# Cached attention on one core: P times V in two 64-row tiles, V loaded with 2 KB rows, and banks shared with the query projection

## Chip, core and metric

The kernel runs on one core of a Trainium2 chip. The metric is the device time of one execution in microseconds. The engines are TensorE (PE, its weight loads listed apart as PEld), VectorE (DVE), ScalarE (ACT), GpSimd (POOL) and SyncE (SP), which issues the loads.

## What is computed

Two independent attention blocks A and B, with the same shapes, everything in bf16:

```python
B, Sq, D = 16, 64, 640
H, Sk, Dh = 32, 512, 128
...
q = (x @ wq).reshape(B, Sq, H, Dh).transpose(0, 2, 1, 3)
scores = jnp.einsum("bhqd,bhkd->bhqk", q, k_cache) * (Dh ** -0.5)
p = _softmax(scores, axis=-1)
o = jnp.einsum("bhqk,bhkd->bhqd", p, v_cache)
return o.transpose(0, 2, 1, 3).reshape(B, Sq, H * Dh) @ wo
```

The output is the two results side by side. Each K and each V cache holds 67 MB, so 268 MB of cache is read once.

## The kernel before

**Tiling.** A step is one head of two batches: 2 x 64 query rows fill the 128 partitions. Two steps (an even and an odd head of the same two batches) make a slot, with number m; there are 256. A group is 16 heads of two batches, 8 slots; a block's 32 heads are done in two passes, the second of which adds the sums of the first. Two slots share one chunk of K and one of V (4 heads), each loaded by two DMAs, one for each batch, into rings of five chunks.

**Stages of a slot**, by the names in the plan and the lines of the emitting code:

- KX (L433, PE): 8 transposes of K for each batch into the K bank; KE (L442, DVE) copies them to SBUF.
- QP2 (L451, PE): 10 matmuls, the query projection of both heads, into bank 6; QE2 (L459, ACT) copies it out, scaled.
- SM2 (L467, PE): 4 matmuls for the scores, each with a 64-column tile of the array, so that the two batches land on the two halves of the partitions. MX (L476, DVE) takes the maxima, EX (L482, ACT) the exponentials and their sums, RC2 (L488, DVE) the reciprocals.
- NM (L496, POOL): P times the reciprocal, one instruction for each head. TR2 (L505, PE): 8 transposes of P into bank 4; TE2 (L512, DVE) copies them out.
- PV2 (L524, PE): P times V, 16 matmuls with 128 keys each (2 heads x 2 batches x 4 key tiles) into bank 5; OE2 (L532, ACT) copies the result out.
- OP2 (L540, L545, PE): the output projection, which sums over a group's 16 heads in banks 0 and 1. At a group's end ACT copies the sum to SBUF (L555, first pass) or DVE adds it to the copy (L560, second pass), and ACT issues the store.
- XT (L604, PE) and XE (L612, ACT) transpose a group's x once, ten slots ahead, in bank 4.

**Order.** Nothing is scheduled at run time. Each engine runs a template once for each iteration k, and the number beside a stage says for which slot, k plus that number, it works:

```python
PE_T = (("TR2", 1), ("QP2", 4), ("KX", 4, 0), ("SM2", 3), ("PV2", 1), ("XT", 0), ("OP2", 0), ("KX", 4, 1))
ACT_T = (("QE2", 4), ("OE2", 1), ("XE", 0), ("EX", 3, 0), ("EX", 3, 1), ("OV", 0), ("ST", -1))
DVE_T = (("TE2", 1), ("RC2", 2), ("KE", 4, 0), ("MX", 3, 0), ("MX", 3, 1), ("KE", 4, 1), ("OVF", 0))
POOL_T = (("NM", 0, 0), ("NM", 0, 1))
```

So PE works on five slots at once. `make_op` lists for each stage the buffers and banks that it reads and writes; from these, in the order of the time stamps `ts`, the plan derives the dependencies, and `prune_waits` drops those that another wait implies. An instruction carries one wait itself; further ones stand as instructions of their own before it. The loads on SP are ordered once, by when their buffer comes free and by when they are due.

**Layout of keys.** K is loaded with 8 consecutive keys for each partition (2 KB in one piece), an even head on partitions 0 to 63 and the odd one on 64 to 127. V is loaded with 4 consecutive keys for each partition (1 KB), one head over all 128. So NM reorders the keys of P as it writes, with every second element, to fit V's order.

Of the kernel before, what the change touches and what calls it, by code (L numbers as in the profile page):

```python
# [14 lines left out]
class Cfg:  # L15
    G = 4
# [9 lines left out]
    NPN = 3  # L26
# [12 lines left out]
class Op:  # L39
# [3 lines left out]
    def __init__(self, eng, kind, idx, reads=(), writes=(), dur=0.0, ts=None, aux=None):  # L43
# [16 lines left out]
          "RC2", "NM0", "NM1", "TR2", "TE2", "XT", "XE", "PV2", "OE2", "OP2", "OV", "ST")  # L60
STAGE_IDX = {s: i for i, s in enumerate(STAGES)}
# [3 lines left out]
def build_plan(dims, cfg):  # L65
# [25 lines left out]
    def mk(eng, kind, idx, reads, writes, stage, m_ts, sub=0, aux=None, dur=0.0):  # L91
        return Op(eng, kind, idx, reads, writes, dur=dur, aux=aux, ts=(m_ts, STAGE_IDX[stage], sub))

# [4 lines left out]
    def make_op(kind, m, sub):  # L98
# [8 lines left out]
        if kind in ("MX", "EX", "NM"):  # L107
# [7 lines left out]
            return mk("pool", "NM", g, [("p", g % cfg.NP), ("recip", r)], [("pn", g % cfg.NPN)], "NM%d" % sub, m, sub)  # L115
        r0, r1 = g0 % cfg.NR, g1 % cfg.NR
        if kind in ("XT", "XE"):
# [4 lines left out]
            m_ts = mt - cfg.XLEAD + OFF["TR2"]  # L122
# [3 lines left out]
        if kind == "QP2":  # L126
            return mk("pe", "QP2", m, [("xT", grp % cfg.NX), ("wq", ps_ % 2, h0 // G)], [("QB",)], "QP2", m)
        if kind == "QE2":
            return mk("act", "QE2", m, [], [("QB",), ("qT", m % cfg.NQ)], "QE2", m)
# [5 lines left out]
        if kind == "TR2":  # L135
            return mk("pe", "TR2", m, [("pn", g0 % cfg.NPN), ("pn", g1 % cfg.NPN), ("ident",)], [("PTB",)], "TR2", m)
        if kind == "TE2":
            return mk("dve", "TE2", m, [], [("PTB",), ("pT", m % cfg.NT)], "TE2", m)
        if kind == "PV2":
            return mk("pe", "PV2", m, [("pT", m % cfg.NT), ("v", c % cfg.NVB, g0 % G), ("v", c % cfg.NVB, g1 % G)],  # L140
                      [("OB",)], "PV2", m)
        if kind == "OE2":
            return mk("act", "OE2", m, [], [("OB",), ("oT", m % cfg.NO)], "OE2", m)
        if kind == "OP2":
            return mk("pe", "OP2", m, [("oT", m % cfg.NO), ("wo", ps_ % 2, h0 // G)], [("OUTB",)], "OP2", m)
        if kind in ("OV", "OVF", "ST"):
# [3 lines left out]
            if kind == "OV":  # L150
                if NHALF == 1:
                    return mk("act", "OV", m, [], [("OUTB",), ("out_sb", grp % 2)], "OV", m, aux=grp)
# [3 lines left out]
            if kind == "OVF":  # L156
                if NHALF == 1 or not last_half:
                    return None
                return mk("dve", "OVF", m, [("outp", bp)], [("OUTB",), ("out_sb", grp % 2)], "OV", m, aux=grp)
            if NHALF == 1 or not last_half:  # L160
                return None
            return mk("act", "ST", m, [("out_sb", grp % 2)], [("out_dram", grp)], "ST", m, aux=grp)
# [3 lines left out]
    for eng, tmpl in templates.items():  # L166
        offs = [t[1] for t in tmpl] + [cfg.XLEAD]
        for k in range(-max(offs), NMAC - min(offs)):
            for t in tmpl:
# [8 lines left out]
                if 0 <= m < NMAC:  # L178
                    op = make_op(kind, m, sub)
                    if op is not None:  # L180
                        progs[eng].append(op)
                        if op.kind == "OV":
                            progs[eng].append(mk("act", "ST", m, [("out_sb", op.aux % 2)], [("out_dram", op.aux)],
# [7 lines left out]
    for ps_ in range(NPASS):  # L191
        first_m = ps_ * MPP
        buf = ps_ % 2
        for j in range(HG):
# [7 lines left out]
            loads.append((rq, m0 - OFF["QP2"], 0, mk("sp", "LDWQ", (ps_, j), [], [("wq", buf, j)], "LDW", m0,  # L202
# [3 lines left out]
    for grp in range(NGRP):  # L206
        m0 = MPG * grp
        op = mk("sp", "LDX", grp, [], [("xn", grp % cfg.NXN)], "LDX", m0 - cfg.XLEAD + OFF["TR2"], aux=grp,
# [35 lines left out]
    def sem_key(op):  # L244
# [6 lines left out]
        if op.kind == "ST":  # L251
            return ("d_out", op.aux % 2)
# [94 lines left out]
def mha_kernel(nc, blocks, out, cfg=None):  # L347
# [30 lines left out]
    with contextlib.ExitStack() as es:  # L378
# [11 lines left out]
        v_ring = sb("v_ring", [128, NVB, 2, G, 4, DH], BF16)  # L390
# [3 lines left out]
        pn_ring = sb("pn_ring", [128, NPN, SK], BF16)  # L394
        pT_ring = sb("pT_ring", [128, NT, 2, 4, 128], BF16)
        oT_ring = sb("oT_ring", [128, NO, 2, 128], BF16)
        out_sb = sb("out_sb", [128, 2, DN], BF16)
# [20 lines left out]
        pt_ps = pt_ps_flat.rearrange("p (s t q) -> p s t q", s=2, t=4)  # L418
        o_ps = ps[:, O_BANK, 0:256]
        q_ps = ps[:, Q_BANK, 0:256]  # L420
# [24 lines left out]
        def em_QP2(e, op):  # L445
            m = op.idx
            first = last = None
            for sub in range(2):
                blk, bp, grp, ps_, hh = step_info(2 * m + sub)
                for kt in range(KT):  # L450
                    ins = e.matmul(q_ps[:, sub * 128:(sub + 1) * 128], wq_sb[:, ps_ % 2, kt, hh * DH:(hh + 1) * DH],  # L451
# [5 lines left out]
        def em_QE2(e, op):  # L457
            m = op.idx
            ins = e.activation(qT_ring[:, m % NQ].rearrange("p s q -> p (s q)"), q_ps, ACTF.Copy, scale=scale)  # L459
# [31 lines left out]
        def em_NM(e, op):  # L491
            g = op.idx
            r = g % NR
            src = p_ring[:, g % NP, :].rearrange("q (th tl pp) -> q th tl pp", th=2, tl=4)
            dst = pn_ring[:, g % NPN, :].rearrange("q (tl pp th) -> q th tl pp", tl=4, th=2)
# [3 lines left out]
        def em_TR2(e, op):  # L499
            m = op.idx  # L500
            first = last = None
            for sub in range(2):
                g = 2 * m + sub
                for t in range(4):
                    ins = e.transpose(pt_ps[:, sub, t, :], pn_ring[:, g % NPN, t * 128:(t + 1) * 128], ident[:, :])  # L505
                    first = first or ins
                    last = ins
            return first, last

        def em_TE2(e, op):  # L510
            m = op.idx
            ins = e.tensor_copy(pT_ring[:, m % NT].rearrange("p s t q -> p (s t q)"), pt_ps_flat)  # L512
            return ins, ins

        def em_PV2(e, op):
            m = op.idx
            first = last = None
            for sub in range(2):
                g = 2 * m + sub
                c, gi = g // G, g % G  # L520
                for j in range(2):
                    for t in range(4):
                        col = sub * 128 + 64 * j
                        ins = e.matmul(o_ps[:, col:col + 64], v_ring[:, c % NVB, j, gi, t, :],  # L524
                                       pT_ring[:, m % NT, sub, t, 64 * j:64 * j + 64], start=(t == 0), stop=(t == 3))
# [4 lines left out]
        def em_OE2(e, op):  # L530
            m = op.idx
            ins = e.activation(oT_ring[:, m % NO].rearrange("p s q -> p (s q)"), o_ps, ACTF.Copy)  # L532
# [16 lines left out]
        def em_OV(e, op):  # L549
            ins = e.activation(out_sb[:, op.aux % 2, :], out_ps_all, ACTF.Copy)  # L550
# [7 lines left out]
        def em_OVF(e, op):  # L558
            blk, bp = grp_info(op.aux)
            ins = e.tensor_tensor(out_sb[:, op.aux % 2, :], out_ps_all, outp[:, bp, :], ALU.add)  # L560
            return ins, ins

        def em_ST(e, op):
            blk, bp = grp_info(op.aux)
            dst = out[2 * bp:2 * bp + 2, :, blk * DN:(blk + 1) * DN].rearrange("b q n -> (b q) n")
            ins = e.dma_start(dst, out_sb[:, op.aux % 2, :])
# [49 lines left out]
        def em_LDKV(e, op):  # L616
# [3 lines left out]
            if op.kind == "LDV":  # L620
# [99 lines left out]
```

## Time and profile before

| | |
|---|---|
| median of 2 runs | 959.13 us (958.80 to 959.47) |
| span of the profiled execution | 956.8 us |
| PE matmuls of KX, L433 | 4096, 220 ns each |
| of PV2, L524 | 4096 of 64 columns, 194 ns each |
| of SM2, L467 | 1024 of 512 columns, 392 ns each |
| ACT copies QE2 (L459) and OE2 (L532) | 256 each, 384 and 383 ns |
| POOL, L496 | 512, 843 ns each, 44% busy |
| DVE copies, L442 and L512 | 691 and 682 ns |
| moved by DMA | 299.51 MB, mean 313 GB/s |
| granted TensorE clock | 0.998 |

The mean duration of a matmul is not its cost: matmuls overlap in the array, and eight of 220 ns that start 56 ns apart are done after 0.61 us. What counts is the distance from start to start. Five slots are under way at once, so a wait names the instruction that came last, and a stage that ends well ahead of its reader costs nothing. The lines of the order of time give the start in us, the time from the first start to the last end, the engine, the line, what is written and read, and how many instructions were merged.

### The profile page before, as it was taken

What the parts mean: (1) busy time and instruction counts of PE and PEld (TensorE: products, weight loads), DVE (VectorE), ACT (ScalarE), POOL (GpSimd) and SP (SyncE); (2) the same over time, 40 slices, a digit from 0 to 9 for tenths busy, and PEclk for the clock granted to TensorE, in tenths of its full rate; (3) what the DMA queues carried; (4) which work ended last, traced back from release to release, by engine and by line L of the source; (5) the groups of instructions that cost most, each with busy time, mean ns of one, the idle gap of its engine ahead of it and who ended that gap; (6) DMA issues with size and microseconds to landing.
All of it is one profiled execution on the core that took longest, in us unless ns stands there. A gap on an engine that the chain in (4) does not pass through costs nothing.

```text
span 956.8 us, 34351 instructions
## 1 busy us (share of the span) xinstructions
PE 919.4 (96%) x14755; PEld 733.5 (77%) x15008; DVE 841.9 (88%) x1552; ACT 567.1 (59%) x1585; POOL 416.9 (44%) x518
## 2 busy tenths in 40 slices
PE   4999999999999999999999999999999999999997
PEld 3877777778777777877777787777877778777775
DVE  2898899898899999899999899889899998999996
ACT  1666656666665565656566666666666656565654
POOL 0444444444444444444444444444444444444443
PEclk9999999999999999999999999999999999999999
DMA  9999999999999999888999999988888988899830
GB/s 315 364 365 364 351 365 367 365 368 351 338 337 337 343 330 315 299 292 305 322 332 352 326 353 327 306 294 296 302 305 288 308 301 297 295 297 314 295 124 15
DMA packets 230871, 299.51 MB, mean 313 GB/s; under 512 B 9536, under 2 KB 165184, under 8 KB 230720
## 3 DMA queue, kind: packets, MB, share of 16 engines
q1 hardware_dynamic: 228416, 294.69, 91.0%
q8 instruction: 118, 1.93, 0.8%
q10 hardware_dynamic: 2304, 2.62, 0.8%
q14 instruction: 33, 0.27, 0.1%
HBM read 294.65 MB, written 2.62 MB: 311 GB/s over the span
## 4 chain that ended last, share of the span: by engine, by line
PE 89%; DVE 4%; POOL 3%; issue 2%; SPq 1%; DMA 1%; POOLq 0%; DVEq 0%
PE ps L433 22%; PE ps L524 14%; PE ps L451 14%; PE ps L467 14%; PE ps L505 12%; PE ps L545 7%; PE ps L540 5%; POOL pn_ring L496 3%; DVE out_sb L560 1%; DVE ktp_ring L442 1%; DVE pT_ring L512 1%; PE ps L604 1%; DMA xn_ring<-in_A_x_dram 1%; SPq L626 1%; SPq L583 1%
## 5 line engine op out<-in xcount | busy, mean ns | idle before, releaser
L496 POOL TENSOR_SCALAR pn_ring<-p_ring,recip 128x512 bf16<-128x512 bf16 x512 | 416.3, 843 | 532.7 <-DVE recip L488 532.7
L442 DVE COPY ktp_ring<-ps 128x1024 bf16<-128x1024 bf16 x512 | 353.7, 691 | 105.3 <-PE ps L433 85.1
L482 ACT ACTIVATE p_ring<-ps,negmax 128x512 bf16<-128x512 f32 x512 | 345.6, 684 | 4.8 <-DVE negmax L476 4.8
L476 DVE TENSOR_REDUCE negmax<-ps 128x1 f32<-128x512 f32 x512 | 327.3, 681 | 0.4 <-PE ps L467 0.3
L433 PE MATMUL ps<-ident,kn_ring 128*128 128x128 bf16 x4096 | 314.6, 220 | 2.8 <-DMA kn_ring<-in_A_k_cache_dram 1.6
L532 ACT ACTIVATE oT_ring<-ps 128x256 bf16<-128x256 f32 x256 | 98.0, 383 | 306.0 <-PE ps L524 306.0
L433 PEld LDWEIGHTS ps<-ident,kn_ring 128*128 128x128 bf16 x4096 | 251.9, 98 | 34.2 <-DVE ktp_ring L442 2.6
L524 PEld LDWEIGHTS ps<-pT_ring,v_ring 128*128 128x128 bf16 x4096 | 133.5, 98 | 109.2 <-issue 100.0
L451 PE MATMUL ps<-xT_ring,wq_sb 128*128 128x128 bf16 x2560 | 186.4, 220 | 3.2 <-DMA wq_sb<-in_A_wq_dram 3.2
L512 DVE COPY pT_ring<-ps 128x1024 bf16<-128x1024 bf16 x256 | 174.5, 682 | 4.6 <-PE ps L505 3.8
L524 PE MATMUL ps<-pT_ring,v_ring 128*128 128x64 bf16 x4096 | 163.8, 194 | 3.3 <-issue 1.7
L467 PE MATMUL ps<-ktp_ring,qT_ring 128*64 128x512 bf16 x1024 | 159.8, 392 | 0.4 <-ACT p_ring L482 0.4
L505 PE MATMUL ps<-ident,pn_ring 128*128 128x128 bf16 x2048 | 156.7, 219 | 3.5 <-POOL pn_ring L496 3.5
L451 PEld LDWEIGHTS ps<-xT_ring,wq_sb 128*128 128x128 bf16 x2560 | 155.2, 98 | 3.5 <-DMA wq_sb<-in_A_wq_dram 3.5
L459 ACT ACTIVATE qT_ring<-ps 128x256 bf16<-128x256 f32 x256 | 98.4, 384 | 66.8 <-PE ps L451 66.8
L505 PEld LDWEIGHTS ps<-ident,pn_ring 128*128 128x128 bf16 x2048 | 124.1, 98 | 7.0 <-POOL pn_ring L496 6.7
L545 PE MATMUL ps<-wo_sb,oT_ring 128*128 128x128 bf16 x512 | 112.1, 219 | 13.4
L482 ACT ACTIVATION_READ_ACCUMULATOR p_ring<-ps,negmax 128x1 f32 x512 | 105.0, 205 | 0.0
L540 PE MATMUL ps<-wo_sb,oT_ring 128*128 128x512 bf16 x259 | 97.8, 379 | 0.0
L540 PEld LDWEIGHTS ps<-wo_sb,oT_ring 128*128 128x128 bf16 x512 | 50.1, 98 | 30.6 <-ACT oT_ring L532 0.3
L467 PEld LDWEIGHTS ps<-ktp_ring,qT_ring 128*64 128x64 bf16 x1024 | 36.1, 108 | 27.1 <-ACT p_ring L482 0.6
L545 PEld LDWEIGHTS ps<-wo_sb,oT_ring 128*128 128x128 bf16 x512 | 50.1, 98 | 0.0
(13 smaller groups left out, 112.7 us busy)
## 6 DMA issues: line engine op xcount, KB each, us to landing
kn_ring<-in_A_k_cache_dram SPq DMA_DIRECT2D x128, 512.0 KB, 7.0
v_ring<-in_A_v_cache_dram SPq DMA_DIRECT2D x128, 512.0 KB, 7.2
kn_ring<-in_B_k_cache_dram SPq DMA_DIRECT2D x126, 512.0 KB, 4.8
v_ring<-in_B_v_cache_dram SPq DMA_DIRECT2D x126, 512.0 KB, 5.7
wq_sb<-in_A_wq_dram SPq DMA_DIRECT2D x8, 640.0 KB, 10.4
wo_sb<-in_A_wo_dram SPq DMA_DIRECT2D x8, 640.0 KB, 10.2
wq_sb<-in_B_wq_dram SPq DMA_DIRECT2D x8, 640.0 KB, 8.4
wo_sb<-in_B_wo_dram SPq DMA_DIRECT2D x8, 640.0 KB, 7.5
```

Source lines behind the costliest of these rows:

```text
L433: ins = e.transpose(kt_ps[:, t8, :], kn_ring[:, c % NKB, j, hp, t8, :], ident[:, :])
L442: ins = e.tensor_copy(dst, src)
L451: ins = e.matmul(q_ps[:, sub * 128:(sub + 1) * 128], wq_sb[:, ps_ % 2, kt, hh * DH:(hh + 1) * DH], xT_ring[:, grp % NX, kt, :], start=(kt ...
L467: ins = e.matmul(s_bank(sub)[64 * j:64 * j + 64, :], qT_ring[:, m % NQ, sub, 64 * j:64 * j + 64], ktp_ring[:, m % NKT, sub, j, :], start=T ...
L476: ins = e.reduce_max(negmax[:, r:r + 1], s_bank(g % 2), axis=AX.X, negate=True)
L482: ins = e.activation(p_ring[:, g % NP, :], s_bank(g % 2), ACTF.Exp, bias=negmax[:, r:r + 1], scale=1.0, accum_out=rowsum[:, r:r + 1])
L496: ins = e.tensor_scalar(dst, src, recip[:, r:r + 1], 1.0, ALU.mult, ALU.mult)
L505: ins = e.transpose(pt_ps[:, sub, t, :], pn_ring[:, g % NPN, t * 128:(t + 1) * 128], ident[:, :])
L512: ins = e.tensor_copy(pT_ring[:, m % NT].rearrange("p s t q -> p (s t q)"), pt_ps_flat)
L524: ins = e.matmul(o_ps[:, col:col + 64], v_ring[:, c % NVB, j, gi, t, :], pT_ring[:, m % NT, sub, t, 64 * j:64 * j + 64], start=(t == 0), s ...
L540: ins = e.matmul(out_ps0, oT_ring[:, m % NO, sub, :], wo_sb[:, ps_ % 2, hh, 0:N0], start=(hh == 0), stop=(hh == SPB - 1))
L545: last = e.matmul(out_ps1, oT_ring[:, m % NO, sub, :], wo_sb[:, ps_ % 2, hh, N0:DN], start=(hh == 0), stop=(hh == SPB - 1))
```

## The change

V is laid out as K is: 8 consecutive keys for each partition, an even head on partitions 0 to 63 and the odd head on 64 to 127. P is normalised into a tile that holds both heads, for each of 8 key tiles 64 keys of the one beside 64 of the other, so that one transpose serves both heads. P times V then runs with 64 keys for each matmul: 32 matmuls instead of 16, alternating between the upper half (even head) and the lower half (odd head) of the array, each named by `tile_position`. The two halves write different banks, 5 and 6; for that the query projection and P times V share both banks, one head in each, and each of the two stages now waits until the other's result was copied out. The output buffer shrinks from two to one, pn becomes two buffers of two heads, and the time stamps count from the reference stage of each part of the pipeline.

```diff
-    NPN = 3
+    NPN = 2
...
+TSREF = dict(KX0="QP2", KE0="QP2", KX1="QP2", KE1="QP2", QP2="QP2", QE2="QP2", LDK="QP2", SM2="SM2", MX0="SM2",
+             MX1="SM2", EX0="SM2", EX1="SM2", RC2="SM2", NM0="SM2", NM1="SM2", TR2="TR2", TE2="TR2", PV2="PV2",
+             OE2="PV2", LDV="PV2", OP2="OP2", OV="OP2", ST="OP2")
...
     def mk(eng, kind, idx, reads, writes, stage, m_ts, sub=0, aux=None, dur=0.0):
+        if stage not in ("LDX", "XT", "XE"):
+            m_ts = m_ts - OFF.get(TSREF.get(stage), 0) + (stage in ("RC2", "NM0", "NM1"))
...
-            return mk("pe", "QP2", m, [("xT", grp % cfg.NX), ("wq", ps_ % 2, h0 // G)], [("QB",)], "QP2", m)
+            return mk("pe", "QP2", m, [("xT", grp % cfg.NX), ("wq", ps_ % 2, h0 // G)], [("QOB",)], "QP2", m)
...
-            return mk("act", "QE2", m, [], [("QB",), ("qT", m % cfg.NQ)], "QE2", m)
+            return mk("act", "QE2", m, [], [("QOB",), ("qT", m % cfg.NQ)], "QE2", m)
...
-                      [("OB",)], "PV2", m)
+                      [("QOB",)], "PV2", m)
...
-            return mk("act", "OE2", m, [], [("OB",), ("oT", m % cfg.NO)], "OE2", m)
+            return mk("act", "OE2", m, [], [("QOB",), ("oT", m % cfg.NO)], "OE2", m)
...
-        v_ring = sb("v_ring", [128, NVB, 2, G, 4, DH], BF16)
+        v_ring = sb("v_ring", [128, NVB, 2, G // 2, 8, DH], BF16)
...
-        pn_ring = sb("pn_ring", [128, NPN, SK], BF16)
-        pT_ring = sb("pT_ring", [128, NT, 2, 4, 128], BF16)
+        pn_ring = sb("pn_ring", [128, NPN, 8, 2, 64], BF16)
+        pT_ring = sb("pT_ring", [128, NT, 8, 128], BF16)
...
-        out_sb = sb("out_sb", [128, 2, DN], BF16)
+        out_sb = sb("out_sb", [128, 1, DN], BF16)
...
-        o_ps = ps[:, O_BANK, 0:256]
-        q_ps = ps[:, Q_BANK, 0:256]
+        pt_ps = pt_ps_flat.rearrange("p (t q) -> p t q", t=8)
+        qo_ps = ps[:, O_BANK:Q_BANK + 1, 0:128]
...
-            src = p_ring[:, g % NP, :].rearrange("q (th tl pp) -> q th tl pp", th=2, tl=4)
-            dst = pn_ring[:, g % NPN, :].rearrange("q (tl pp th) -> q th tl pp", tl=4, th=2)
+            src = p_ring[:, g % NP, :].rearrange("q (t pp) -> q t pp", t=8)
+            dst = pn_ring[:, (g // 2) % NPN, :, g % 2, :]
             ins = e.tensor_scalar(dst, src, recip[:, r:r + 1], 1.0, ALU.mult, ALU.mult)
...
-            for sub in range(2):
-                g = 2 * m + sub
-                for t in range(4):
-                    ins = e.transpose(pt_ps[:, sub, t, :], pn_ring[:, g % NPN, t * 128:(t + 1) * 128], ident[:, :])
+            for t in range(8):
+                ins = e.transpose(pt_ps[:, t, :], pn_ring[:, m % NPN, t].rearrange("q h p -> q (h p)"), ident[:, :])
...
-            for sub in range(2):
-                g = 2 * m + sub
-                c, gi = g // G, g % G
-                for j in range(2):
-                    for t in range(4):
-                        col = sub * 128 + 64 * j
-                        ins = e.matmul(o_ps[:, col:col + 64], v_ring[:, c % NVB, j, gi, t, :],
-                                       pT_ring[:, m % NT, sub, t, 64 * j:64 * j + 64], start=(t == 0), stop=(t == 3))
+            c, hp = 2 * m // G, (2 * m % G) // 2
+            for j in range(2):
+                for t in range(8):
+                    for sub in range(2):
+                        r0 = 64 * sub
+                        ins = e.matmul(qo_ps[:, sub, 64 * j:64 * j + 64], v_ring[r0:r0 + 64, c % NVB, j, hp, t, :],
+                                       pT_ring[r0:r0 + 64, m % NT, t, 64 * j:64 * j + 64],
+                                       start=(t == 0), stop=(t == 7), tile_position=(r0, 0))
...
-            if op.kind == "LDV":
-                src = blocks[blk][2][2 * bp + j, h0 + hlo:h0 + hhi].rearrange("g (p t) d -> p g t d", p=128)
-                ins = e.dma_start(v_ring[:, c % NVB, j, hlo:hhi], src)
-            else:
...
+            cache, ring = (blocks[blk][2], v_ring) if op.kind == "LDV" else (blocks[blk][1], kn_ring)
+            src = cache[2 * bp + j, h0 + hlo:h0 + hhi].rearrange("(hp hs) (p t) d -> (hs p) hp t d", hs=2, t=8)
+            ins = e.dma_start(ring[:, c % NKB, j, hlo // 2:hhi // 2], src)
```

## The prediction

> **What bounds the kernel now.** I read the page first, in the order busy shares, chain, groups; then the waits; then the instructions in order of time between 400 and 412 us.
>
> ```profile
> PE 919.4 (96%) x14755; PEld 733.5 (77%) x15008; DVE 841.9 (88%) x1552; ACT 567.1 (59%) x1585; POOL 416.9 (44%) x518
> ...
> PE 89%; DVE 4%; POOL 3%; issue 2%; SPq 1%; DMA 1%; POOLq 0%; DVEq 0%
> ...
> L524 PEld LDWEIGHTS ps<-pT_ring,v_ring 128*128 128x128 bf16 x4096 | 133.5, 98 | 109.2 <-issue 100.0
> ...
> L467 PEld LDWEIGHTS ps<-ktp_ring,qT_ring 128*64 128x64 bf16 x1024 | 36.1, 108 | 27.1 <-ACT p_ring L482 0.6
> ...
> kn_ring<-in_A_k_cache_dram SPq DMA_DIRECT2D x128, 512.0 KB, 7.0
> v_ring<-in_A_v_cache_dram SPq DMA_DIRECT2D x128, 512.0 KB, 7.2
> ```
>
> PE is on 89% of the chain that ended last. A busy PE alone would not prove that the array is full, so the order of time decides:
>
> ```profile
> 400.26 0.64 PE L524 MATMUL ps<-pT_ring,v_ring 128*128 128x64 bf16 x16
> ...
> 400.74 0.44 PE L604 MATMUL ps<-ident,xn_ring 128*128 128x128 bf16 x5
> ...
> 403.01 0.61 PE L433 MATMUL ps<-ident,kn_ring 128*128 128x128 bf16 x8
> ...
> 403.21 0.38 ACT L459 ACTIVATE qT_ring<-ps 128x256 bf16<-128x256 f32 x1
> ...
> 403.55 0.62 PE L467 MATMUL ps<-ktp_ring,qT_ring 128*64 128x512 bf16 x4
> ...
> 404.10 0.52 PEld L524 LDWEIGHTS ps<-pT_ring,v_ring 128*128 128x128 bf16 x16 [0.41 <-issue]
> 404.11 0.64 PE L524 MATMUL ps<-pT_ring,v_ring 128*128 128x64 bf16 x16
> ...
> 404.79 0.38 ACT L532 ACTIVATE oT_ring<-ps 128x256 bf16<-128x256 f32 x1 [1.19 <-PE ps L524]
> ...
> 405.13 0.61 PE L433 MATMUL ps<-ident,kn_ring 128*128 128x128 bf16 x8
> 405.58 0.61 PE L505 MATMUL ps<-ident,pn_ring 128*128 128x128 bf16 x8
> ...
> 405.97 0.60 PEld L451 LDWEIGHTS ps<-xT_ring,wq_sb 128*128 128x128 bf16 x10
> ...
> 407.12 0.62 PE L467 MATMUL ps<-ktp_ring,qT_ring 128*64 128x512 bf16 x4
> ```
>
> From L467 to the next L467 is 407.12 - 403.55 = 3.57 us: one slot, two heads of two batches. L433 starts every (0.61 - 0.219)/7 = 0.056 us; eight make 0.45, and L505 follows exactly 405.58 - 405.13 = 0.45 later. So between full-array groups the array has no gap. L524 starts every (0.64 - 0.193)/15 = 0.029-0.030 us; sixteen make 0.47, and L604 follows 0.48 after it: no gap either. But L433 to L467 is 403.55 - 403.01 = 0.54, which is 0.45 plus a gap of 0.09. L467's second pair starts at 0.62 - 0.38 = 0.24, and its 512 columns take 0.22 (L540 to L545, 401.29 to 401.51), so the array is free at 404.01 and L524 starts at 404.11: a gap of 0.10. Nothing is late there: the weights' idle time is "issue". These two gaps are where 64-column tiles begin and end.
>
> Whole run: 3.57 x 256 = 914; 30 slots with L604 add 0.28 each, 8; 16 slots with the vector add L560 stretch their two periods to 404.11-407.86-411.75, that is 3.75 and 3.89, 0.5 more than twice 3.57, 8 in all. Head and tail make the rest of the 956.8 us span. The median of the runs is 959.1, 2.3 above the span; I carry that difference over. Each 0.01 us a slot is 2.5 us, counting 250 slots (the first are paced by loads, the last three by the softmax chain).
>
> **The change part by part.** *P-times-V matmuls.* 16 matmuls of 128 rows become 32 of 64 rows, in pairs on the upper and lower half of the array; each still streams 64 columns. If a pair runs side by side, 16 pairs keep the 0.029 pace and the block stays 0.47. L467 shows side-by-side tiles: within the first 0.41 us after 403.55 lie two of its 512-column matmuls, though one alone lasts 0.39. That is for column halves; row halves no row shows. Each pair also needs two weight loads of 128 columns. The trace's first two L524 loads end 0.11 apart from the first's start, so the second began 0.11 - 0.098 = 0.015 after the first; two, one after the other, are 0.03 a pair, just the pace of the matmuls. I add 0.013 for the block. Bounds: 0 if the loads hide; a gain is excluded, since a half-array tile streams as many columns; above, no overlap, 32 x 0.0292 = 0.93, +0.47.
>
> The Trainium skill, "TensorE: Matmul & The Clock Gate", Part 3, gives about 4 ns between starts of packed tiles; by it, as an estimate, a pair would cost 0.033 and the total would be some 13 us higher than mine. Its Weight-path section ties the fast weight load to 128 columns, not to rows, which no run here shows for a 64-row tile.
>
> *A third change of tile shape.* Before, PE goes full, columns, full: two gaps a slot, 0.09 and 0.10. After, it goes full, columns, rows, full: PV2 to OP2 (or XT) is new. The nearest rows are these two gaps, so I take 0.095, plus 0.010 because the first load can no longer run ahead (L524's first matmul lasts 203 ns instead of 193): 0.105 a slot. Lower bound 0, if only column tiles cost it; a gain is excluded, as PV2 to OP2 has no gap now. This is the largest term.
>
> "TensorEngine Tiling (Array Packing)", Key Properties, says that changing the tiling mode, not just the tile, drains the engine; it speaks against the change and gives no figure. By it the new gap must come, and with the measured size the sum is mine; without it the sum is the second case below.
>
> *Shared banks.* QP2 now waits for OE2, with KX0, SM2 and all behind it in PE's queue. OE2 ends 404.79 + 0.38 = 405.17, QP2 starts 405.97: 0.80 spare. PV2 waits for QE2, with OP2, KX1 and TR2 behind it: QE2 ends 403.21 + 0.38 = 403.59, PV2 starts 404.10: 0.51 spare. In slots where ACT copies partial sums at L555, QE2 ends at 59.56 and PV2 starts at 59.85: 0.29 spare. Cost 0; without the spare each 0.1 us late is 25 us. QE2 and OE2 now read two banks; same size, 0.38 each, ACT is 59% busy.
>
> *The normalising (NM).* Its writes become runs of 64 instead of every second element. POOL takes 2 x 0.81 a slot and is 44% busy; I take no change. A gain is worth at most the 8 us of the L560 slots, where PE waits for it; slower by over 0.24 us a slot (it ends 405.28, TR2's loads start 405.52) it would enter the loop. TR2 and TE2 keep 8 transposes and one copy.
>
> *V's transfers.* As many DMAs of the same 512 KB, 2 KB per row as K has now: median 7.0 us to landing against 7.2. PE waits for DMAs only at the start, some 12 us in all. Gain 0 to 1, I take 0; a V load slower than K's would have five chunks of cover.
>
> *One answer together:* the output buffer goes from two to one (a store lands in 5.6 us, the next group comes after eight slots, 28 us), two buffers of pn for pairs replace three singles, and the time stamps change only the order in which dependencies are found: 0. If the output buffer's cover were gone, 16 stores of 5.6 us bound it.
>
> *Given back.* In L560 slots DVE is the late one (0.81 more on 3.50 of work in 3.57). Slots longer by 0.118 give back 2 x 0.118 x 16 = 4 us.
>
> Sum: 0.105 + 0.013 = 0.118 x 250 = 29.5; minus 4; 956.8 + 25.5 + 2.3 = 985. With a pair at 0.030 to 0.040 instead, and the gap 0.09 to 0.105, the span of this case is 975 to 1028.
>
> **The rivals.** *The gap is the column tiles' own (not slower).* Both gaps now touch L467, and L467's 64-column load lasts 108 ns against 98 for 128 columns, so it is the odd one. If row tiles cost no gap, 0.013 x 250 = 3, minus up to 8 from L560 slots if NM gets quicker: 953 to 962. It decides once the new gap is under 0.06 (0.073 x 250 - 2 = 16). Against it: the second gap stands before full-array work, whose loads were free to run ahead.
>
> *The halves do not overlap, or loads go slowly.* Serial matmuls cost 0.93 a block. So do slow loads: L467's take about 0.03 for 64 columns (0.14 busy for four, less 0.108), hence 0.06 for 128, times 16 = 0.93. So does the queue, if it cannot pass PE's instructions faster than L524's 32 in 0.47, since there are now 64. All give (0.47 + 0.105) x 250 = 143, less the 8: 1094. For it: no row shows 64-row tiles. Against: L467's pairs overlap, and its four instructions start within 0.01.
>
> *QE2 ends last before PV2.* If ACT took 0.1 more than its spare, 1010. Against: 0.51 spare in nearly all slots.
>
> *PE gets shorter* would need fewer streamed columns; nothing removes any.
>
> **How the numbers follow.** Third gap with overlapping halves 0.58; no gap 0.20; no overlap 0.17; late QE2 0.03; faster for a reason not seen 0.02. About 2% (19 us, to 978) is what a measurement can tell. Slower by over 2%: 0.54 of the first (its low end falls inside), 0.17 and 0.03: 0.74. Within: 0.20 + 0.04 = 0.24. Faster: 0.02. The range takes the first two cases and the late QE2, 953 to 1028, some 0.80, and leaves out no overlap and faster. The likeliest case's own range is 975 to 1028.
>
> **What would show it.** A slot of 3.68 to 3.70 us; a gap of about 0.1 between the last PV2 matmul and L545's group; PV2's 32 matmuls within 0.65, starting in pairs; no wait of PE for ACT; periods at L560 slots only 0.3 above two slots. PV2 lasting 1.1 us would make the sum wrong by the third case; a slot of 3.57 to 3.60 by the second; PE waiting for oT_ring or qT_ring would show the shared banks.

## The result, and the profile after

| | before | after |
|---|---|---|
| median | 959.13 us | 989.55 us (986.73 to 992.36, 2 runs) |
| ratio | | 1.0315 [1.0284, 1.0346] |
| span of the profiled execution | 956.8 us | 985.0 us (device time 986.73) |
| distance from L467 (after: L472) to the next, normal slot | 3.57 us | 3.67 us |
| POOL, NM | 843 ns | 695 ns |
| share of the load queue q1 in the DMA engines' time | 91.0% | 85.3% |

Slower by 3%, and slower by the route that the forecast took. From the page of the kernel after: busy time by engine, the queues, the chain that ended last, three groups and two DMA issues.

```profile
PE 959.3 (97%) x19104; PEld 748.4 (76%) x19104; DVE 842.2 (86%) x1552; ACT 571.1 (58%) x1585; POOL 349.9 (36%) x518
...
q8 instruction: 151, 2.47, 1.0%
...
PE 93%; DVE 3%; SPq 1%; issue 1%; DMA 1%; POOL 0%; POOLq 0%; ACT 0%; DVEq 0%
...
L501 POOL TENSOR_SCALAR pn_ring<-p_ring,recip 128x512 bf16<-128x512 bf16 x512 | 349.3, 695 | 627.8 <-DVE recip L493 627.8
...
L526 PEld LDWEIGHTS ps<-pT_ring,v_ring 64*128 64x128 bf16 x8192 | 134.4, 95 | 111.6 <-issue 104.6
...
L472 PEld LDWEIGHTS ps<-ktp_ring,qT_ring 128*64 128x64 bf16 x1024 | 36.1, 108 | 27.2 <-ACT p_ring L487 0.6
...
kn_ring<-in_A_k_cache_dram SPq DMA_DIRECT2D x128, 512.0 KB, 5.5
v_ring<-in_A_v_cache_dram SPq DMA_DIRECT2D x128, 512.0 KB, 6.3
```

PE's share of the chain rose from 89 to 93%: no other engine became the bound. The loads got easier and land sooner, and nothing waits for that. PE's busy time rose by 40 us, which says little: it is the union of overlapping records, and the records before were a few per cent short (14755 of 15008 matmuls). One slot in order of time says more:

```profile
402.24 0.62 PE L472 MATMUL ps<-ktp_ring,qT_ring 128*64 128x512 bf16 x4
402.80 0.64 PE L526 MATMUL ps<-pT_ring,v_ring 64*128 64x64 bf16 x32
403.37 0.39 PE L543 MATMUL ps<-wo_sb,oT_ring 128*128 128x512 bf16 x1
403.60 0.22 PE L548 MATMUL ps<-wo_sb,oT_ring 128*128 128x128 bf16 x1
...
405.92 0.62 PE L472 MATMUL ps<-ktp_ring,qT_ring 128*64 128x512 bf16 x4
406.47 0.64 PE L526 MATMUL ps<-pT_ring,v_ring 64*128 64x64 bf16 x32
407.04 0.39 PE L543 MATMUL ps<-wo_sb,oT_ring 128*128 128x512 bf16 x1
```

The 32 matmuls of 64 rows (L526) take the 0.64 us that the 16 of 128 rows took. In the single records two start 3 ns apart and the next two 29 ns after these, 0.450 us from the first start to the last, against 0.447 before. But L543 starts 0.57 after the block's start. From L526's last start to L543's is 0.122; before, 0.029 was enough from L524 to L604 (in most other slots the record of the first L540 is missing). That is the third gap, 0.093 us. L543's first matmul lasts 390 ns instead of 379, 0.010 more. L545's records are all there, and they say the same of a slot without L604: before, its first matmul starts 0.69 after the block's start (404.11), after (L548) 0.80.

```profile
404.80 0.22 PE L545 MATMUL ps<-wo_sb,oT_ring 128*128 128x128 bf16 x1
```

The other two changes of shape are as they were: 149 ns from the last of K's transposes to the scores, 312 ns from the last score matmul to P-times-V. The normal slot grew by 0.107 us, 3.674 instead of 3.567.

This, 252 times, makes 27.0 of the 28.2 us that the span grew by. The rest has two parts, both in PE's row. The first is an idle PE that waits for no semaphore ("issue"), here after L548:

```profile
133.97 0.38 PE L543 MATMUL ps<-wo_sb,oT_ring 128*128 128x512 bf16 x1
134.19 0.22 PE L548 MATMUL ps<-wo_sb,oT_ring 128*128 128x128 bf16 x1
135.27 0.62 PE L438 MATMUL ps<-ident,kn_ring 128*128 128x128 bf16 x8 [0.86 <-issue]
```

From L548 to L438 is 0.056 elsewhere; here it is 1.08. There are 13 such stalls, 0.2 to 1.0 us each, 5.7 us together, and none before. The instruction at which PE goes on has the same number each time, counted from PE's first and modulo 256. A 16 KB packet of the instruction queue q8 started 2.2 to 2.7 us ahead of each. 256 instructions in 16 KB are 64 bytes for one, and the 151 packets of q8 (118 before) go with PE's 38208 matmuls and weight loads (2 x 15008 = 30016 before). So I read these stalls as PE at the end of a page of instructions whose successor isn't there yet; the median distance from one 16 KB packet to the next is 6.4 us instead of 7.8.

The second part goes the other way. Before, a slot with the vector add lost 0.18 at P-times-V (behind TE2) and 0.32 at TR2 (behind NM). After, it loses 0.27, all at P-times-V, and again behind TE2 (L515), which follows the vector add (L563) on DVE:

```profile
898.74 0.81 DVE L563 TENSOR_TENSOR out_sb<-ps,outp 128x640 bf16<-128x640 f32 x1
...
899.14 0.39 ACT L464 ACTIVATE qT_ring<-ps 128x256 bf16<-128x256 f32 x1 [0.37 <-PE ps L456]
899.48 0.68 DVE L515 COPY pT_ring<-ps 128x1024 bf16<-128x1024 bf16 x1
...
900.30 0.64 PE L526 MATMUL ps<-pT_ring,v_ring 64*128 64x64 bf16 x32 [0.20 <-DVE pT_ring L515]
```

TE2 ends at 900.16, just ahead of P-times-V; QE2 (L464) was done at 899.53. The view of the waits has two lines that look alike (us, times, longest):

```profile
PEld ps L526 <- ACT qT_ring L464: 6.6, 16, 0.4
...
PE ps L526 <- DVE pT_ring L515: 3.0, 15, 0.2
```

The first lies in 15 slots with ACT's copy of the first pass and one at the start. Its 0.41 is the idle time that any L526 load has, so QE2 costs nothing there. The second is the loss. Fifteen slots with 0.24 less give 3.6 us back (the sixteenth addition falls in the tail). Head, first three slots and tail are 1.0 shorter. Together 27.0 + 5.7 - 3.6 - 1.0 = 28.1 of 28.2.

### The profile page after: what moved, and what is told of

It reads as the page before. It is cut to its first block, busy times and chain, and to the rows that moved or that the text cites. A ratio compares the mean times of both kernels' runs of the same rounds, so it can differ in the third digit from the quotient of the medians.

```text
span 985.0 us, 42919 instructions
## 1 busy us (share of the span) xinstructions
PE 959.3 (97%) x19104; PEld 748.4 (76%) x19104; DVE 842.2 (86%) x1552; ACT 571.1 (58%) x1585; POOL 349.9 (36%) x518
## 3 DMA queue, kind: packets, MB, share of 16 engines
q1 hardware_dynamic: 162880, 294.69, 85.3%
## 4 chain that ended last, share of the span: by engine, by line
PE 93%; DVE 3%; SPq 1%; issue 1%; DMA 1%; POOL 0%; POOLq 0%; ACT 0%; DVEq 0%
PE ps L438 22%; PE ps L526 15%; PE ps L456 14%; PE ps L543 14%; PE ps L472 13%; PE ps L508 11%; PE ps L548 3%; PE ps L607 1%; DVE out_sb L563 1%; DVE ktp_ring L447 1%; DVE pT_ring L515 1%; DMA xn_ring<-in_A_x_dram 1%; SPq L625 1%; SPq L586 0%; POOL pn_ring L501 0%
## 5 line engine op out<-in xcount | busy, mean ns | idle before, releaser
L501 POOL TENSOR_SCALAR pn_ring<-p_ring,recip 128x512 bf16<-128x512 bf16 x512 | 349.3, 695 | 627.8 <-DVE recip L493 627.8
L438 PE MATMUL ps<-ident,kn_ring 128*128 128x128 bf16 x4096 | 314.7, 220 | 4.0 <-DMA kn_ring<-in_A_k_cache_dram 1.5
L438 PEld LDWEIGHTS ps<-ident,kn_ring 128*128 128x128 bf16 x4096 | 251.8, 98 | 36.0 <-DVE ktp_ring L447 2.6
L526 PEld LDWEIGHTS ps<-pT_ring,v_ring 64*128 64x128 bf16 x8192 | 134.4, 95 | 111.6 <-issue 104.6
L515 DVE COPY pT_ring<-ps 128x1024 bf16<-128x1024 bf16 x256 | 174.4, 681 | 4.3 <-PE ps L508 4.3
L526 PE MATMUL ps<-pT_ring,v_ring 64*128 64x64 bf16 x8192 | 164.7, 191 | 5.6 <-DVE pT_ring L515 3.0
L543 PE MATMUL ps<-wo_sb,oT_ring 128*128 128x512 bf16 x512 | 169.0, 384 | 0.0
L472 PE MATMUL ps<-ktp_ring,qT_ring 128*64 128x512 bf16 x1024 | 159.9, 392 | 0.4 <-DVE ktp_ring L447 0.4
L464 ACT ACTIVATE qT_ring<-ps 128x256 bf16<-128x256 f32 x256 | 98.7, 385 | 87.9 <-PE ps L456 87.9
L548 PE MATMUL ps<-wo_sb,oT_ring 128*128 128x128 bf16 x512 | 112.1, 219 | 0.5 <-issue 0.4
L543 PEld LDWEIGHTS ps<-wo_sb,oT_ring 128*128 128x128 bf16 x512 | 49.7, 97 | 41.8 <-ACT oT_ring L535 0.2
L472 PEld LDWEIGHTS ps<-ktp_ring,qT_ring 128*64 128x64 bf16 x1024 | 36.1, 108 | 27.2 <-ACT p_ring L487 0.6
L548 PEld LDWEIGHTS ps<-wo_sb,oT_ring 128*128 128x128 bf16 x512 | 50.3, 98 | 0.7 <-issue 0.7
## 6 DMA issues: line engine op xcount, KB each, us to landing
wo_sb<-in_A_wo_dram SPq DMA_DIRECT2D x8, 640.0 KB, 10.3
```

Of the source, the lines that this page charges most:

```text
L438: ins = e.transpose(kt_ps[:, t8, :], kn_ring[:, c % NKB, j, hp, t8, :], ident[:, :])
L472: ins = e.matmul(s_bank(sub)[64 * j:64 * j + 64, :], qT_ring[:, m % NQ, sub, 64 * j:64 * j + 64], ktp_ring[:, m % NKT, sub, j, :], start=T ...
L501: ins = e.tensor_scalar(dst, src, recip[:, r:r + 1], 1.0, ALU.mult, ALU.mult)
L515: ins = e.tensor_copy(pT_ring[:, m % NT].rearrange("p t q -> p (t q)"), pt_ps_flat)
L526: ins = e.matmul(qo_ps[:, sub, 64 * j:64 * j + 64], v_ring[r0:r0 + 64, c % NVB, j, hp, t, :], pT_ring[r0:r0 + 64, m % NT, t, 64 * j:64 * j ...
L543: ins = e.matmul(out_ps0, oT_ring[:, m % NO, sub, :], wo_sb[:, ps_ % 2, hh, 0:N0], start=(hh == 0), stop=(hh == SPB - 1))
```

## The experiments

**The theory.** Each change between full-array, column and row tiles costs PE about 0.09 us, and 64-row matmuls pair up without loss. Rivals: the gap is the column tiles' own, or belongs to the end of the P-times-V block; the shared banks or the loads cost part of it. Beside these: what the stalls are, and what the change holds that is worth keeping.

**The kernel after once more** (no edit), to see whether the stalls are fixed in place.

> The changed kernel once more, for its spread. Its profile shows twelve stalls of PE of 0.2 to 1.0 us in places without a wait, 5.7 us in all, and before shows none; its two runs lie 5.6 us apart, those of before 0.7. If the stalls are late instructions that depend on what the load traffic does in each run, the runs lie between 984 and 994 and differ by several us, and the stalls are in other places in this profile. If they belong to places in the program, the stalls come back in the same places and the runs lie within 1 us.

989.19 us (986.07 to 994.93, 4 runs), ratio 1.0318 [1.0282, 1.0355]. The profile had 15 stalls, 7.7 us, in a device time of 989.31; after's had 5.7 in 986.73. So 2.0 of the 2.6 us between the two executions are stalls. Nine of the 15 came at the same ends of pages as in the first profile, the others at other ends, and all at the same number modulo 256: the places where a stall can come are fixed, whether one comes is not. The runs of the kernel before lay within 1.8 us (7 runs), these within 9.

**One full-array matmul at the end of the block**, and **the same matmul between its two batches**. It streams 8 columns and writes columns that nothing reads.

```diff
+            last = e.matmul(ps[:, O_BANK, 256:264], ident[:, :], pT_ring[:, m % NT, 0, 0:8], start=True, stop=True)
```

```diff
+                if j == 0:
+                    e.matmul(ps[:, O_BANK, 256:264], ident[:, :], pT_ring[:, m % NT, 0, 0:8], start=True, stop=True)
```

> The changed kernel plus one matmul of 8 columns on the full array after the 32 tiled ones of P times V, with the same number of changes of tile shape a slot (three). All theories: the small matmul costs about 0.03 us a slot, 250 x 0.03 = 7 us, so 992 to 1000. It is the control of the next run; its result goes to an unused part of bank 5 and is not read.

> The same small matmul, but in the middle of the 32 tiled ones, between the two batches: the array goes rows, full, rows, two more changes of shape a slot. Each change costs 0.094 plus 0.010 for the load that cannot run ahead (my theory): 0.21 a slot more than the control, +52 us, about 1048. Rival one, the 0.094 belongs to the end of the P times V block, whatever its shape: the same time as the control within 5 us. Rival two, only column tiles cost a change: also the same as the control.

At the end: 997.50 us, ratio 1.0404 [1.0385, 1.0424]. In the middle: 1036.85 us, 1.0813 [1.0794, 1.0832]. One slot of each in order of time, first the matmul (L531) at the end:

```profile
404.00 0.64 PE L526 MATMUL ps<-pT_ring,v_ring 64*128 64x64 bf16 x32
404.57 0.18 PE L531 MATMUL ps<-pT_ring,ident 128*128 128x8 bf16 x1
404.61 0.38 PE L544 MATMUL ps<-wo_sb,oT_ring 128*128 128x512 bf16 x1
```

then the matmul (L532) in the middle:

```profile
400.24 0.41 PE L526 MATMUL ps<-pT_ring,v_ring 64*128 64x64 bf16 x16
400.58 0.18 PE L532 MATMUL ps<-pT_ring,ident 128*128 128x8 bf16 x1
400.69 0.41 PE L526 MATMUL ps<-pT_ring,v_ring 64*128 64x64 bf16 x16
401.03 0.39 PE L545 MATMUL ps<-wo_sb,oT_ring 128*128 128x512 bf16 x1
```

At the end the gap stands ahead of L531, 0.122 from the last L526, and next to none is left before L544 (0.039 instead of 0.029). In the middle the last L526 of a batch to L532 is 0.122, L532 to the next L526 is 0.112, and the end keeps its 0.122. The work is the same; two more changes of shape lengthen the slot from 3.70 to 3.89, 0.19 us (I had written 0.21). That is 0.095 for each change, in a place that has nothing to do with the column tiles or the end of the block: both of those rivals are out. Over 250 slots 0.191 makes 48; the profiled spans differ by 45.0, with 3.3 us less in stalls. The medians differ by 39.4: the profiled execution with the matmul at the end was the fastest of its four, the one with it in the middle the slowest.

"TensorEngine Tiling (Array Packing)" in the Trainium skill, Key Properties, says that changing the mode drains TensorE; these two runs agree, in that PE loses time at each change, and give it a price here, 0.083 to 0.095 us.

**The two row halves one after the other.** Eight key tiles of the upper half, then eight of the lower.

```diff
-                for t in range(8):
-                    for sub in range(2):
+                for sub in range(2):
+                    for t in range(8):
```

> The changed kernel with the 32 tiled matmuls in another order: for each batch all eight of the upper half, then all eight of the lower half, so that neighbours share a half. If two matmuls run side by side only when neighbours use different halves, the block grows from 0.47 to 0.92 or 0.93 us, +0.45 x 250 = +113, about 1102. If the two halves run side by side in any order, 985 to 994. If the alternation had not bought anything, also no change.

1024.53 us, ratio 1.068 [1.0659, 1.0701]: slower, but far less than the 1102 that I wrote down. The block in order of time:

```profile
401.78 0.81 PE L526 MATMUL ps<-pT_ring,v_ring 64*128 64x64 bf16 x32
402.52 0.39 PE L543 MATMUL ps<-wo_sb,oT_ring 128*128 128x512 bf16 x1
```

From the first to the last start it takes 0.617 us, not the 0.905 of 32 in single file, nor the 0.450 of pairs. The single starts are 0, 39, 69, 98, 127, **135**, 156, **174**, 185, **203**, 214 ns and on: two strands with 29 ns steps, of which the second begins while the first is still in its eight. The records don't name the half. But steps under 29 ns are seen in no other P-times-V block than those that alternate halves, so the second strand must be the lower half's: its first matmul starts before three of the upper half's eight. So matmuls for the idle half were taken ahead of ones that stand before them in the program. That is an inference; if it holds, it is why the run missed. What the run does show is that order matters: alternating the halves, as the change does, is worth 0.17 us a slot over this.

**The change's plan and banks with the old layout.** The new dependencies, time stamps, shared banks for QP2 and PV2, one output buffer and pn in pairs; V, NM's strided write and the 16 full-array matmuls stay.

```diff
-            return mk("pe", "QP2", m, [("xT", grp % cfg.NX), ("wq", ps_ % 2, h0 // G)], [("QB",)], "QP2", m)
+            return mk("pe", "QP2", m, [("xT", grp % cfg.NX), ("wq", ps_ % 2, h0 // G)], [("QOB",)], "QP2", m)
...
-        out_sb = sb("out_sb", [128, 2, DN], BF16)
+        out_sb = sb("out_sb", [128, 1, DN], BF16)
```

> The changed kernel's plan, with its shared banks' waits (QP2 waits for OE2, PV2 for QE2), its two pn buffers of two heads and its one output buffer, but before's layout: full-array P times V with 16 matmuls, 1 KB rows of V, NM with every second element, and separate banks 5 and 6. My theory: the slot stays 3.57 us, as both waits have 0.5 us or more to spare, and only the 16 slots with the vector add move, by 0.2 either way: 955 to 963. Rival, the shared waits cost the time: 980 or more, with PE waiting for ACT in most slots.

958.46 us (10 runs) against 958.62 (17 runs): ratio 1.0002 [0.9993, 1.0011]. The normal slot stays 3.57 us. In the L560 slots the two waits changed their sizes:

```profile
PEld ps L511 <- POOL pn_ring L502: 5.7, 17, 0.9
...
PE ps L530 <- DVE pT_ring L518: 3.0, 15, 0.2
```

P-times-V loses 0.27 there, behind TE2, instead of 0.18, and TR2 0.25 behind NM instead of 0.32: together 0.52, before 0.51. P-times-V starts 0.15 after TE2's end here, 0.14 in after and 0.06 before. In these two the wait for TE2 is an instruction of its own ahead of the first load, which carries the wait for QE2; that this makes the 0.09 is not shown. In any case the shared banks cost nothing in the normal slot, and PE never waited for QE2.

**V in 1 KB rows.** Each V load is split into two of 4 keys for each partition, layout and matmuls as after.

```diff
+            if op.kind == "LDV":
+                src, dst = src[:, :, 4 * th:4 * th + 4], dst[:, :, 4 * th:4 * th + 4]
+            ins = e.dma_start(dst, src)
```

> The changed kernel with each load of V split in two that take 1 KB of each row, so the rows are as short as before and nothing else of the compute changes. The slot stays 3.67 in all theories. If PE's stalls without a wait are late instructions behind a load queue that is full, they become more, since the loads need longer to catch up: 988 to 1000, with more than 5.7 us of stalls. If the stalls have nothing to do with the loads, 985 to 992.

**No V loads after the first five chunks**, so that later slots multiply with the V of the first ones.

```diff
+            if kind == "LDV" and c >= n_ring:
+                continue
```

> The changed kernel without the loads of V after the first five chunks: the later slots multiply with V of the first ones, so the output is not the reference's; every compute instruction stays. The loads fall by nearly half. If PE's stalls are late instructions behind the loads, they vanish, and the time falls by some 5.7 to 8 us against the changed kernel of the same chip, to 979 to 983, with runs within 1.5 us of each other. If the stalls come from the sequencer or the number of instructions alone, they stay and the time is 984 to 993.

With 1 KB rows 991.87 us (990.24 to 993.19), ratio 1.0345 [1.0332, 1.0359]; without most V loads 984.31 (983.72 to 984.99), 1.0268 [1.0254, 1.0281]. The slot is 3.67 in both, so the slot's 0.107 doesn't come from V's transfers. The stalls move: 21 of them, 10.3 us, in the first; 6, 4.1 us, in the second. I had expected none there, and missed. Its stretches of time, with the DMA engines' share as the last but one column, show where they stayed:

```profile
40.00:72.00 32.00, 30.14 (x597) 23.12 (x595) 25.77 (x49) 18.34 (x52) 10.86 (x16) 1.00 1.07 372
72.00:290.00 218.00, 218.00 (x4392) 170.63 (x4390) 191.20 (x354) 130.79 (x365) 80.11 (x118) 1.00 0.54 188
...
500.00:510.00 10.00, 8.80 (x172) 6.90 (x170) 7.11 (x14) 5.71 (x17) 2.71 (x4) 1.00 0.65 235
510.00:980.00 470.00, 465.89 (x9375) 363.47 (x9372) 411.12 (x760) 277.27 (x773) 171.14 (x252) 1.00 0.41 141
```

Four fall in 40 to 72 us, two in 500 to 510, where the second block's weights and first chunks come in; at shares of 0.54 and 0.41 there is none in some 690 us, though the pages are as many. The kernel after has the same picture: its last stall is at 617 us, and from 620 on its DMA share is 0.76. A busy DMA alone isn't enough either: the kernel before has 1.07 in 30 to 150 us and no stall. So stalls were seen only where pages are needed often, most of them where the DMA engines are busy; but the share alone doesn't decide: 0.65 had two here, while 0.91 from 136 to 311 us and the 0.76 in the kernel after had none. Why q8's packet isn't started earlier stays open; no run here changes only the number of instructions.

**What is worth keeping: NM without the stride.** In after NM takes 695 ns instead of 843. Two ways to have that without the row tiles were tried. The first keeps K and loads V with two DMAs of 64 partitions each, so that NM writes runs.

```diff
-                src = blocks[blk][2][2 * bp + j, h0 + hlo:h0 + hhi].rearrange("g (p t) d -> p g t d", p=128)
-                ins = e.dma_start(v_ring[:, c % NVB, j, hlo:hhi], src)
+                src = blocks[blk][2][2 * bp + j, h0 + hlo:h0 + hhi].rearrange("g (pp th t) d -> th pp g t d", th=2, t=4)
+                ins = e.dma_start(v_ring[64 * th:64 * th + 64, c % NVB, j, hlo:hhi], src[th])
```

> Before with one part of the change: NM writes runs of 64 elements instead of every second one. V's keys are put on other partitions for it (two loads of 64 partitions for each one of 128, 1 KB rows as before), so the result is the reference's. NM takes 695 ns instead of 843 as in the changed kernel; the slot stays 3.57, and in the 16 slots with the vector add the second delay (0.32, PE waiting for NM) goes, the first (0.18, PE waiting for the transposed P) stays: 16 x 0.32 = 5 us less, 953 to 956. Rival: DVE alone sets those slots, or the halved loads cost at the start: 957 to 962.

1244.40 to 1294.07 us in six runs; the two fastest, 1244.40 and 1259.05, give the ratio 1.3057 [1.2997, 1.3117]. NM falls to 691 ns, but what that is worth the run doesn't say, since the loads became the bound. The page, packets and chain, of the execution of 1294.07:

```profile
DMA packets 235001, 299.55 MB, mean 232 GB/s; under 512 B 13664, under 2 KB 169312, under 8 KB 234848
...
DMA 60%; SPq 20%; PE 17%; issue 1%; DVE 0%; POOL 0%; POOLq 0%; DVEq 0%
```

232 GB/s instead of 313 for the same bytes (over the fastest run's span of 1242.4 us they would make 241); a 1 KB packet took 81 ns on average instead of 50. The run with V in 1 KB rows has as many V loads, of the same 256 KB, and packets of the same sizes, but each of its loads goes to all 128 partitions:

```profile
DMA packets 235034, 300.09 MB, mean 303 GB/s; under 512 B 13664, under 2 KB 169312, under 8 KB 234848
```

There a 1 KB packet took 49 ns. So neither the short rows nor the halved loads do it; by exclusion it is the 64 partitions of each load, though the two kernels differ in more than their loads.

The second way gives K the layout of V, 4 keys for each partition over all 128. Then K's and V's keys have the same order, and neither NM nor KE reorders anything.

```diff
-        kn_ring = sb("kn_ring", [128, NKB, 2, G // 2, 8, DH], BF16)
+        kn_ring = sb("kn_ring", [128, NKB, 2, G, 4, DH], BF16)
...
-            src = p_ring[:, g % NP, :].rearrange("q (th tl pp) -> q th tl pp", th=2, tl=4)
-            dst = pn_ring[:, g % NPN, :].rearrange("q (tl pp th) -> q th tl pp", tl=4, th=2)
+            src, dst = p_ring[:, g % NP, :], pn_ring[:, g % NPN, :]
```

> Before with K loaded in V's layout (4 keys for each partition, 1 KB rows, one DMA as before), so that P's columns stand in V's order: NM and the copy of K write plain runs, and nothing is reordered. NM 695 ns instead of 843 as in the changed kernel, the slot 3.57. In the 16 slots with the vector add PE's wait for NM (0.32) goes and the wait for the transposed P (0.18) stays: 953 to 956 (the loads take 1 KB rows throughout, 49 ns for 1 KB against 94 for 2 KB, some 20 us more of each DMA engine's time, hidden while PE is the bound). Rival: DVE alone sets those slots and the time stays 958 to 960; or the shorter rows delay the start, 960 to 964.

954.60 us (953.76 to 954.94) against 958.76: ratio 0.9953 [0.994, 0.9965]. From its page, the load queue and NM:

```profile
q1 hardware_dynamic: 293952, 294.69, 96.5%
...
L494 POOL TENSOR_SCALAR pn_ring<-p_ring,recip 128x512 bf16<-128x512 bf16 x512 | 349.5, 696 | 594.6 <-DVE recip L487 594.6
```

NM is down to 696 ns, and the slots with the vector add lose 0.25 instead of 0.5; 16 x 0.25 = 4. This is NM's speed alone, at an unchanged slot. The loads, all with 1 KB rows now, take 96.5% instead of 91.0% of the DMA engines' time and still hold nothing up.

**The vector add off DVE.** ACT copies the second pass's sum out of PSUM, rounded to bf16, and POOL adds: alone, and with K's new layout.

```diff
-    DVE_T = (("TE2", 1), ("RC2", 2), ("KE", 4, 0), ("MX", 3, 0), ("MX", 3, 1), ("KE", 4, 1), ("OVF", 0))
-    POOL_T = (("NM", 0, 0), ("NM", 0, 1))
+    DVE_T = (("TE2", 1), ("RC2", 2), ("KE", 4, 0), ("MX", 3, 0), ("MX", 3, 1), ("KE", 4, 1))
+    POOL_T = (("NM", 0, 0), ("NM", 0, 1), ("OVF", -2))
...
```

> Before, with the vector add of the second pass (0.81 us on DVE, 16 slots) taken from DVE: ACT copies the group's sum out as bf16, and POOL adds the first pass's sum to it. The second pass's sum is rounded to bf16 before the addition. If the 16 slots lose 0.5 us each because DVE is late there, the loss goes and the time falls by up to 8 us: 950 to 953. Rival: ACT's copy (0.7) or POOL's add makes QE2 or NM as late as DVE was: 957 to 960.

> Both of the last two together. If each takes a different part of the 8 us that the 16 slots lose, 949 to 952, below both kernels; if both take the same part, as the vector add alone: 950 to 953.

Both missed: 968.69 us, ratio 1.0102 [1.0089, 1.0116], and 964.39, 1.0057 [1.0043, 1.0071]. POOL and the slot's TR2 in the first of the two, in order of time:

```profile
289.08 1.41 POOL L560 TENSOR_TENSOR out_sb<-out_sb,outp 128x640 bf16<-128x640 bf16 x1 [1.89 <-ACT out_sb L550]
...
290.47 1.63 POOL L496 TENSOR_SCALAR pn_ring<-p_ring,recip 128x512 bf16<-128x512 bf16 x2
...
292.16 0.62 PE L505 MATMUL ps<-ident,pn_ring 128*128 128x128 bf16 x8 [0.95 <-POOL pn_ring L496]
```

POOL's addition takes 1.41 us where DVE's took 0.81, and it stands just ahead of NM, whose input is there at 289.0. So TR2 waits 0.95 for P. One slot later in POOL's list, behind that NM, it falls into an idle time of about 2 us (this run has K's new layout too):

```diff
+    POOL_T = (("NM", 0, 0), ("NM", 0, 1), ("OVF", -3))
```

> The kernel before, with K in 1 KB rows and NM written in runs (as the run with K in V's layout), and the vector add of the 16 L560 slots done by an ACT copy of PSUM and a POOL addition that is placed one slot later than in the two runs that put it in front of NM (the second pass's sum is rounded to bf16 before the addition). Those two waited 0.95 us for NM in each of these slots, because POOL's addition takes 1.41 us and stood ahead of NM. My theory: behind the next slot's NM the addition lies in POOL's idle time of about 2 us, DVE has no addition left, and these slots lose nothing or 0.05 us instead of 0.25: 16 x 0.25 = 4 us below the 954.6 of the run without the addition's move, 950 to 952. Rival: ACT's copy (about 0.7 us) delays the query projection's copy or the exponential that P-times-V waits for, or POOL's addition still holds up an NM: 954 to 962.

952.00 us (951.21 to 952.42, 5 runs) against 959.08: ratio 0.9924 [0.9911, 0.9938]. POOL in order of time:

```profile
290.18 1.36 POOL L494 TENSOR_SCALAR pn_ring<-p_ring,recip 128x512 bf16<-128x512 bf16 x2 [2.20 <-DVE recip L487]
291.51 1.41 POOL L558 TENSOR_TENSOR out_sb<-out_sb,outp 128x640 bf16<-128x640 bf16 x1
293.75 1.37 POOL L494 TENSOR_SCALAR pn_ring<-p_ring,recip 128x512 bf16<-128x512 bf16 x2 [0.84 <-DVE recip L487]
```

After the addition POOL still idles 0.84. The slots with the addition are 3.57 like the others. At the last slot this execution is 3.1 us ahead of the one that only has K's new layout, and 1.3 of these go again: from there to the end of the span it takes 12.8 us instead of 11.5, because ACT's copy and POOL's addition (0.71 + 1.41) stand there in place of DVE's 0.81. This is the fastest version here, 0.8% below the kernel before; its interval lies just below that of K's new layout alone.

## Why the prediction was right

- **The third change of shape** (0.105 a slot): right in place and size, 0.093 for the gap and 0.010 for a longer first matmul, in nearly every one of 256 slots. Taking the two gaps already in the trace as the price of a third was the step that carried the forecast, and the matmul in the middle of the block confirmed it.
- **The block of P-times-V** (+0.013): mis-sized. It measured 0.003. I had the second load of a pair wait for 0.015 us; in fact pairs keep the 29 ns pace and start 3 ns apart. The weight load of a 64-row tile takes 95 ns, a full one's 98, and none of it shows. By that term the sum was 2.5 us too high. The 4 ns between starts of packed tiles, from "TensorE: Matmul & The Clock Gate", Part 3, in the Trainium skill, agree with the 3 ns inside a pair; but pairs follow each other at 29 ns, not 33, so the higher total that I worked out from that page doesn't hold.
- **Missing from the sum: instruction pages.** Doubling the matmuls and weight loads of one stage makes 27% more PE instructions. I considered the queue's pace, not the fetch: 5.7 us in the profiled execution, 7.7 in another. The trace of before had no such stall, so its rows gave no price, but q8's row counts the packets. The two errors, 2.5 too much and 5.7 too little, partly cancel; that the sum came so near is in part luck.
- **Given back in the L560 slots** (4 us): the size was right (3.6), the mechanism wrong; that is luck. I had DVE profit from a longer slot. But the wait behind DVE's TE2 grew from 0.18 to 0.27, as much as in the kernel with the old layout at a slot of 3.57. The addition starts 0.74 us before the next scores in both kernels (406.38 to 407.12, 898.74 to 899.48): it stands behind KE, which waits for K's last transposes, and these move with the slot. What went is the other wait, TR2's 0.32 for NM, and two instructions of NM now take 1.36 us instead of 1.63. The check that I named, 0.3 above two slots, came true in its number (0.27).
- **NM "no change"**: wrong, 843 to 695 ns. POOL has slack in all but the L560 slots, and there it is what gave the 4 us back: the kernel with K's new layout, at an unchanged slot, gains as much.
- **Shared banks at 0**: right; the kernel with the old layout gave 1.0002 [0.9993, 1.0011]. The third rival, QE2 last before P-times-V, is seen in no slot.
- **V's transfers at 0**: right in effect. The loads use less of the DMA engines' time, and PE waited for them only at the start. Going back to 1 KB rows lengthens no slot; it adds some stalls.
- **The rivals.** The column tiles alone and no overlap are out by the slot (3.67, just below the 3.68 to 3.70 that I named) and the block (0.64).

The median stands 4.6 above my 985, as the profiled span 985.0 has a device time of 986.73 and the other run was at 992.36; between the two profiled executions of this kernel the stalls made most of the distance.

## What to carry to other kernels

Here, with an array that is hardly ever idle, every change between full, row and column tiles cost about 0.1 us: look at the gaps around the odd-shaped group, take them as the price, and count how many changes a slot has before and after. Splitting a matmul into halves that run side by side left the array's time as it was here (0.450 us against 0.447), but doubles its instructions, and these have to be fetched while the loads run. A wait that a view names may be idle time that every slot has: compare its length with the others' before it is called a loss. Where a change bundles a layout with a cheaper operation, look for the other layout that gives the operation alone: here K could follow V instead of V following K.

## What was not expected of the hardware

- PE can run out of instructions: stalls of 0.2 to 1.2 us at a fixed place modulo 256 instructions, when a page was needed every 6.4 us, most of them while the DMA engines were busy. "Runtime: NRT & Kernel Launch" in the Trainium skill says that 16 KiB blocks of 256 instructions are refilled while the engine runs, at a cost that is mostly hidden. Here it was hidden at all but 13 and 15 of 151 pages in the two executions of the kernel after.
- Matmuls of the other row half appear to be taken some three places early: 0.617 us for a block that would take 0.905 in single file.
- V loads split into two of 64 partitions: 232 GB/s over the span, against 303 with as many loads of that size over 128 partitions.
- POOL's write of every second bf16 element cost 21% (843 against 695 ns); DVE's copies of K took 692 ns with and without reordering.
